# Scores from 64-row halves, batch 0's K and Q kept on chip, and a new place for the first six search steps

## The chip, the cores and the metric

The kernel runs on one core of one Trainium2 chip. The metric is the device time of one launch in microseconds: 1080.16 us, the median of three runs (1077.16 to 1082.32). A profile of one more execution, with its trace, is what the text below reads.

## The reference, cut to what matters

```python
# q, k, v: [4 batches, 8 heads, 576 tokens, 64]
scores = q @ k.T / 8
kth = the 32nd largest of each row
attn = softmax(scores where scores >= kth, else -1e9)
x = (attn @ v), as [2304 tokens, 512]
h = x @ w_in;            x = max(0.01 * h, h) @ w_out        # 512 -> 2048 -> 512
h = max(x @ w1, x @ w2, x @ w3);  out = h @ w_out2           # 512 -> 768 -> 512
```

Everything is float32 or wider at the boundary; the weights come as float64 bits.

## The kernel before

Every operand of a matmul is split into two float16 parts, a high and a low one, so that products keep nearly float32 accuracy: three or four matmuls for one.

**Attention** works in *steps*. The tokens of a batch are cut into four full blocks of 128 (F0 to F3) and a half block of 64 (HB); the heads come in four pairs (`hp`). A full step is one block and one head pair: 128 query rows, both heads side by side, 576 scores each. A half step is the half block and two head pairs: 64 rows of one head and 64 of another share the 128 partitions. Batch 0 goes F0, HB, F1, F2, F3, so its steps 0 to 3 are F0, 4 and 5 are HB, and 6 to 17 are F1 to F3. There are 72 steps, 64 of them full. One step (`attention`, L685):

- TensorE makes the scores of head j=0 into PSUM (L707), ScalarE evicts them into S (L712), then the same for j=1. There is one score buffer in PSUM and three S buffers.
- VectorE searches the 32 largest of each row: MAX8 (L722) four times and MATCH_REPLACE8 (L724) three times, for both heads. A head's search starts when its own eviction is done.
- ScalarE and POOL make the exponentials, their sums' factors and the high and low parts (L732 to L756); a DMA transposes them (L757); TensorE multiplies by V (L783 to L785); ScalarE scales by the row sum.
- When a block's last head pair is done, a second DMA transposes its tokens into the buffer of a *unit* (`xu<-xhl`, L819).

In the scores both halves of q and k are stacked on the 128 contraction rows: for one head, k's tile holds the high part in rows 0 to 63 and the low part in rows 64 to 127, and q's tile is there twice, once as high over low and once as low over high (`st`). Two matmuls of 128 rows then give all four products. To get these layouts, `prep_qk` (L372) splits q and k of each batch and head pair, writes the parts to DRAM (L394, two DMAs each), and `load_k` (L411, one DMA) and `load_q` (L419, L422, three DMAs per block) read them back.

**Units** are the token groups of the feed-forward part (`ffn`, L846), ten of them: 192 tokens (F0 and HB of batch 0), 128 (F1), then 256 (unit 2 is F2 and F3 of batch 0) seven times, and 192. A unit does `h<-xu,wi` and `acc<-f16t,wo` (the first two matrices), then `h<-k,w` and `acc<-f16t,w` (the other two stages), 672 matmuls in all, three for each product (`three`, L824). Unit 0 waits for all of `w_in` and `w_out`, and its second half for all of the others.

**Weights** come as float64 and are converted on VectorE in chunks, three integer operations for 512 columns (L501, L504, L507), then scaled and split by ScalarE and POOL (`prep_w`, L475). `prep_w` is called for 8 chunks of `w_in`, 8 of `w_out`, 6 of w1 to w3 and 4 of the last matrix.

**Order.** All this is entered into a planner (`Plan`, L75) as operations with an engine, an estimated length, what they read and write, and a priority. The planner lays the operations out by these estimates, engine by engine, taking what can start earliest and among those the lower priority; the program then has that order on every engine, and each engine works through its list in order. A search step i has priority TP(i) (L678): 0, 2, 4 and 6 for the first NE=4 steps, then 10 + 11.9 i, which is 57.6 and 69.5 for steps 4 and 5. The chunks have priorities from 2.0 on, 2.1 apart for `w_in` (to 16.7), 1.5 for `w_out` (18.8 to 29.3), and end near 47. So steps 4 and 5 stand behind all weights.

SP issues all DMAs from one list, in order.

Of the kernel before, what the change touches and what calls it, by code (L numbers as in the profile page):

```python
# [36 lines left out]
VC = 11  # L37
# [15 lines left out]
NE = 4  # L53
TE = 0.0
TS = 2.0
# [5 lines left out]
class Buf:  # L61
    def __init__(self, tag, make):
        self.tag, self.make, self.ap, self.left, self.seq, self.also = tag, make, None, 0, None, ()
        self.done, self.emit = None, 0
        self.last = 0.0
# [9 lines left out]
class Plan:  # L75
# [50 lines left out]
    def run(self):  # L126
# [11 lines left out]
        while len(order) < total:  # L138
            best = None
            for e, lst in pend.items():  # L140
                t0 = free[e]
                cand = None
                for n in lst:
                    t, ok = max(n.ready, t0, lanes[-8] if e == SP else 0.0), True
                    need = {}
                    for b in n.bufs:
                        if b.ap is None and b.last == 0.0 and not getattr(b, "on", False):
# [6 lines left out]
                            t = max(t, sl[k] + 0.2)  # L154
                    if not ok:
# [78 lines left out]
def attention_moe_kernel(ctx, tc, qk, v, w_in, w_out, w123, w2o, outT):  # L234
# [9 lines left out]
    NB = {"xu": 2, "raw": 2, "hl": 1, "k2": 7, "kt": 4, "qt": 2, "vt": 4, "S": 3, "w": 1, "m": 2, "nb": 2, "nt": 2, "pp": 1,  # L244
# [46 lines left out]
    NCOL = 318  # L291
# [80 lines left out]
    def prep_qk(b, hp, pr, fast):  # L372
        d = dr.tile([2, 2, 2, D, S], F16, name=f"dqk{b}_{hp}")
# [3 lines left out]
        for a in (1, 0):  # L377
# [31 lines left out]
    def load_k(b, hp, pr):  # L409
        k = buf("kt", [P, 2, S], F16)  # L410
        op(SP, 0.55, lambda: Y.dma_start(k(), DQK[b, hp][1].rearrange("h r d s -> (r d) h s")),  # L411
           r=[("d", b, hp, 1, 0), ("d", b, hp, 1, 1)], w=[k], pr=pr, dma=dma(P * 2 * S * 2))
        KT[b, hp] = k

    def load_q(b, hp, t0, n, pr):
        q = buf("qt", [P, 2, 2, P], F16)
        rd = [("d", b, hp, 0, 0), ("d", b, hp, 0, 1)]
        src = DQK[b, hp][0]
# [724 lines left out]
```

## Time and profile before

| | |
|---|---|
| median of three runs | 1080.16 us |
| the profiled execution's own time | 1078.56 us |
| its span on the core | 1076.6 us |
| TensorE (PE) busy | 903.1 us, 84% |
| VectorE (DVE) busy | 875.2 us, 81% |
| ScalarE (ACT) busy | 835.2 us, 78% |
| GpSimd (POOL) busy | 600.5 us, 56% |
| DMA, all queues | 125.78 MB, mean 117 GB/s |

Times in rows are microseconds from the span's start, unless marked ns. L707 is line 707 of the kernel before. A matmul's row gives its start and how long it was in flight; matmuls overlap, so the rate is read from start to start. `128*128` or `128*64` in a matmul's row is the part of the array that it uses: contraction rows by output columns. PEld is TensorE's weight load, SPq the queue of SP that issues DMAs. The page's slices are fortieths of the span, about 27 us each.

### The profile page before, as it was taken

How to read it: one execution, taken by the hardware profiler on the slowest of the kernel's cores; microseconds unless marked ns; L12 is line 12 of the kernel's file. 1: busy time of each engine (PE TensorE's matmuls, PEld its weight loads, DVE VectorE, ACT ScalarE, POOL GpSimd, SP SyncE). 2: the span in 40 equal slices, each digit the busy share in tenths (PEclk: the TensorE clock that was granted, in tenths of full speed). 3: DMA queues.
4: the chain of work that ended last, by engine and by line, in shares of the span. 5: the costliest groups of instructions: out<-in, count | busy, mean ns of one | idle time of the engine just before them, and what ended most of it. 6: DMA issues, size and time to landing. Idle time of an engine off the chain costs nothing.

```text
span 1076.6 us, 27391 instructions
## 1 busy us (share of the span) xinstructions
PE 903.1 (84%) x10292; PEld 795.0 (74%) x10292; DVE 875.2 (81%) x2010; ACT 835.2 (78%) x1769; POOL 600.5 (56%) x1110
## 2 busy tenths in 40 slices
PE   3343334688999998998999899989999999999998
PEld 2231223577988887887888798878878897888998
DVE  5899999999998999999459999999389999900101
ACT  7777878999888888689879868987887788664242
POOL 5355766776476655467655545666754555443131
PEclk9985556789999999999999999999999999999999
DMA  8968447547755443355763334663833343220000
GB/s 283 310 147 277 162 110 247 158 111 150 129 106 118 100 89 68 77 125 127 143 173 82 80 76 98 155 123 88 173 80 88 79 90 85 65 60 2 21 2 16
DMA packets 268516, 125.78 MB, mean 117 GB/s; under 512 B 237408, under 2 KB 255328, under 8 KB 266336
## 3 DMA queue, kind: packets, MB, share of 16 engines
q1 hardware_dynamic: 268384, 124.04, 47.4%
q8 instruction: 81, 1.33, 0.5%
q14 instruction: 51, 0.42, 0.1%
HBM read 62.65 MB, written 14.16 MB: 71 GB/s over the span
## 4 chain that ended last, share of the span: by engine, by line
PE 42%; ACT 18%; DVE 10%; DMA 7%; POOL 6%; issue 5%; SPq 1%; POOLq 0%; ACTq 0%; DVEq 0%
PE h L825 7%; PE h L826 7%; PE h L827 7%; PE acc L825 5%; PE acc L826 5%; PE acc L827 5%; DMA pt<-phl 3%; DVE m L722 3%; PE s L707 3%; POOL phl L754 3%; DVE w L724 3%; ACT pp L749 3%; ACT pp L746 2%; ACT S L712 2%; DMA raw<-in_v 2%
## 5 line engine op out<-in xcount | busy, mean ns | idle before, releaser
L722 DVE MAX8 m<-w 128x8 f32<-128x576 f32 x432 | 308.8, 748 | 0.3
L886 POOL TENSOR_TENSOR f16t<-k,f16t 128x256 f16<-128x256 f32 (+2 forms) x220 | 136.9, 624 | 211.2 <-ACT f16t L880 193.1
L754 POOL TENSOR_TENSOR phl<-pp,phl 128x576 f16<-128x576 f32 x144 | 183.5, 1282 | 85.3 <-ACT phl L752 83.2
L724 DVE MATCH_REPLACE8 w<-m,w 128x576 f32<-128x576 f32 x288 | 212.4, 743 | 0.0
L825 PE MATMUL h<-k,w 128*128 128x256 f16 (+2 forms) x720 | 186.4, 263 | 7.7 <-ACT k L926 5.5
L826 PE MATMUL h<-k,w 128*128 128x256 f16 (+2 forms) x720 | 186.3, 263 | 3.4 <-POOL k L928 3.0
L827 PE MATMUL h<-k,w 128*128 128x256 f16 (+2 forms) x720 | 186.3, 263 | 0.0
L826 PE MATMUL acc<-f16t,wo 128*128 128x256 f16 (+2 forms) x640 | 165.8, 263 | 3.7 <-POOL f16t L886 3.7
L825 PE MATMUL acc<-f16t,wo 128*128 128x256 f16 (+2 forms) x640 | 166.0, 263 | 0.7 <-ACT f16t L880 0.6
L827 PE MATMUL acc<-f16t,wo 128*128 128x256 f16 (+2 forms) x640 | 165.9, 263 | 0.0
L825 PE MATMUL h<-xu,wi 128*128 128x256 f16 (+1 forms) x576 | 155.9, 271 | 3.2 <-DMA xu<-xhl 1.9
L827 PE MATMUL h<-xu,wi 128*128 128x256 f16 (+1 forms) x576 | 156.0, 271 | 0.0
L826 PE MATMUL h<-xu,wi 128*128 128x256 f16 (+1 forms) x576 | 156.0, 271 | 0.0
L707 PE MATMUL s<-kt,qt 128*128 128x288 f16 (+5 forms) x800 | 106.2, 281 | 46.1 <-ACT S L712 31.8
L746 ACT ACTIVATE pp<-S,nt 128x576 f32<-128x576 f32 x144 | 107.9, 771 | 32.7 <-POOL nt L732 24.8
L880 ACT ACTIVATE f16t<-k 128x256 f16<-128x256 f32 (+2 forms) x220 | 86.9, 396 | 56.3 <-DVE k L970 53.7
L749 ACT ACTIVATE pp<-pp,nb,colt 128x576 f32<-128x576 f32 x144 | 123.7, 866 | 0.1
L722 DVE MAX8 m<-S 128x8 f32<-128x576 f32 x144 | 103.5, 746 | 19.1 <-ACT S L712 19.0
L707 PEld LDWEIGHTS <-qt 128*128 128x128 f16 (+1 forms) x800 | 62.3, 106 | 66.3 <-issue 41.9
L873 ACT ACTIVATE k<-h,colt 128x256 f32<-128x256 f32 (+2 forms) x160 | 72.4, 455 | 48.0 <-PE h L827 47.4
L826 PEld LDWEIGHTS <-w 128*128 128x128 f16 x960 | 94.2, 98 | 17.4 <-issue 9.2
L724 DVE MATCH_REPLACE8 w<-m,S 128x576 f32<-128x576 f32 x144 | 106.4, 743 | 0.0
(132 smaller groups left out, 2507.6 us busy)
## 6 DMA issues: line engine op xcount, KB each, us to landing
rw<-in_w SPq DMA_DIRECT2D x18, 512.0 KB, 5.5
w<-in_w_in SPq DMA_DIRECT2D x8, 1024.0 KB, 7.2
w<-in_w_out SPq DMA_DIRECT2D x8, 1024.0 KB, 5.6
raw<-in_qk SPq DMA_DIRECT2D x24, 288.0 KB, 3.5
dqk<-hl SPq DMA_DIRECT2D x48, 144.0 KB, 2.7
kt<-dqk SPq DMA_DIRECT2D x16, 288.0 KB, 3.0
qt<-dqk SPq DMA_DIRECT2D x144, 32.0 KB, 2.2
raw<-in_v SPq DMA_DIRECT2D x12, 352.0 KB, 3.4
```

The costliest lines, as they stand in the source:

```text
L707: T.matmul(p()[osl, h, o:o + w], q()[:, hh, st, :n], k()[:, hh, kc:kc + w], start=st == 0, stop=st == 1, skip_group_check=True)
L722: op(DVE, dve(S), lambda mc=mc, src=src: V.max(mc(), src()), r=rd, w=[(m, j, 0, r)], pr=pd)
L724: op(DVE, dve(S) + 0.06, lambda mc=mc, src=src, j=j: V.match_replace(out=wp()[:, j], in_to_replace=mc(), in_values=src(), imm_value=NEG), ...
L746: op(ACT, act(S, aps=1), lambda j=j: A.activation(pp()[:, j], Sb[j](), AF.Prelu, bias=nt()[:, j:j + 1], alpha=STEEP), r=[(Sp, j), nt], w=[ ...
L749: op(ACT, act(S, aps=2), lambda j=j, es=es: A.activation(pp()[:, j], pp()[:, j], AF.Exp, bias=nb()[:, j:j + 1], scale=es), r=[(nb, j), ((" ...
L754: op(POOL, pool(S), lambda j=j: G.tensor_tensor(phl()[:, 1, j], pp()[:, j], phl()[:, 0, j], op=ALU.subtract), r=[(pp, j), (phl, 0, j)], w= ...
L825: T.matmul(out, wt(0), xt(0), start=first, stop=False, skip_group_check=True)
L826: T.matmul(out, wt(0), xt(1), start=False, stop=False, skip_group_check=True)
L827: T.matmul(out, wt(1), xt(0), start=False, stop=last, skip_group_check=True)
L873: op(ACT, act(N, True, 1), lambda: A.activation(rr()[:, 0, :N], p()[:, :N], AF.Prelu, scale=SC["e"][:, c:c + 1], alpha=0.01), r=[p, "e_in" ...
L880: op(ACT, act(N), lambda: A.activation(hl()[:, 0, :N], g()[:, 0, :N], AF.Copy), r=[(g, 0)], w=[(hl, 0)], pr=pr)
L886: op(POOL, pool(N), lambda: G.tensor_tensor(hl()[:, 1, :N], g()[:, 0, :N], hl()[:, 0, :N], op=ALU.subtract), r=[(g, 0), (hl, 0)], w=[(hl, ...
```

## The change

- **Scores.** k's and q's tiles now have both heads of a pair on the 128 rows, head 0 in rows 0 to 63 and head 1 in rows 64 to 127, and the high and the low part side by side. One matmul contracts over 64 rows; four of them (high and low of q by high and low of k, `x` and `y`) add up in PSUM. The score group is now one half of the columns (`c`, 288) of both heads instead of all columns of one: for a full step 8 matmuls of 288 columns, the heads in turn, for a half step 16. The eviction takes a column half of both heads, and a head's search starts when both evictions are done. In half steps the two partition halves belong to two head pairs and not to two heads of one; their scale factors are put into one column by two small POOL copies.
- **Columns.** The second head's keys are rotated by 64 tokens on the host, as the kernel before did by three matmuls of 64, 224 and 288 columns. V loses one of 11 padded column groups.
- **DRAM round trips.** The parts are written in one DMA instead of two, q's block is read in one instead of three. For batch 0, k's parts stay in the buffer that the scores read, and nothing is written or read; q's parts are read where they lie for the first block (F0) and go through DRAM for the other four.
- **Plan.** The first six steps get the priorities 0, 4, 8, 12, 16 and 20 (NE=6, TS=4.0), so steps 4 and 5 stand among the last chunks of `w_in` and the first of `w_out`. And an operation that uses a buffer which another has already taken is not laid out before the buffer came free (`since`).

```diff
-VC = 11
+VC = 10
-NE = 4
+NE = 6
-TS = 2.0
+TS = 4.0
...
+                        else:
+                            t = max(t, b.since)
...
-                    slots[b.tag].pop(0)
+                    b.since = slots[b.tag].pop(0) + 0.2
...
 def prep_qk(b, hp, pr, fast):
-        d = dr.tile([2, 2, 2, D, S], F16, name=f"dqk{b}_{hp}")
+        d = dr.tile([2, P, 2, S], F16, name=f"dqk{b}_{hp}")
...
-            hl = buf("hl" if b else "ph", [P, 2, S], F16)
+            hl = buf("hl" if b else "kt" if a else "ph", [P, 2, S], F16)
...
-            for h in range(2):
-                op(SP, 0.55, lambda hl=hl, a=a, h=h: Y.dma_start(d[a, h].rearrange("r d s -> d r s"),
-                                                               hl()[h * D:(h + 1) * D]),
-                   r=[(hl, 0), (hl, 1)] + z0, w=[("d", b, hp, a, h)], pr=pr, dma=dma(P * S * 2))
+            if b == 0 and a:
+                KT[b, hp] = hl
+                continue
+            if b == 0:
+                QT[b, hp, ORDER[0][0][0]] = hl
+            op(SP, 0.55, lambda hl=hl, a=a: Y.dma_start(d[a], hl()), r=[(hl, 0), (hl, 1)] + z1, w=[("d", b, hp, a)],
+               pr=pr, dma=dma(P * 2 * S * 2))
...
 def load_q(b, hp, t0, n, pr):
-        q = buf("qt", [P, 2, 2, P], F16)
-        op(SP, 0.55, lambda: Y.dma_start(q()[:, :, 0, :n], src[:, :, :, t0:t0 + n].rearrange("h r d s -> (r d) h s")),
-           r=rd, w=[(q, 0)], pr=pr, dma=dma(P * 2 * n * 2) + 0.2)
-        for r in range(2):
-            op(SP, 0.55, lambda r=r: Y.dma_start(q()[r * D:(r + 1) * D, :, 1, :n],
-                                                src[:, 1 - r, :, t0:t0 + n].rearrange("h d s -> d h s")),
-               r=rd, w=[(q, 1 + r)], pr=pr, dma=dma(P * n * 2) + 0.2)
+        if (b, hp, t0) in QT:
+            return
+        q = buf("qt", [P, 2, P], F16)
+        op(SP, 0.55, lambda: Y.dma_start(q()[:, :, :n], DQK[b, hp][0][:, :, t0:t0 + n]), r=[("d", b, hp, 0)],
+           w=[(q, 0), (q, 1)], pr=pr, dma=dma(P * 2 * n * 2) + 0.2)
...
 def attention(i):
-        for j in range(2):
-            k, q = KT[b, hps[j]], QT[b, hps[j], t0]
+        pairs = [(slice(0, n), hps[0])] if full else [(slice(0, 64), hps[0]), (slice(64, P), hps[1])]
...
+        for c in range(2):
             p = buf("s", [P, 2, 512])
-            hs = [(j, slice(0, P))] if full else [(0, slice(0, 64)), (1, slice(64, P))]
-            cols = ((0, 0, 0, 288), (1, 0, 288, 288)) if j == 0 else \
-                   ((0, 0, 512, 64), (0, 64, 0, 224), (1, 0, 224, 288))
-            def qk_(p=p, k=k, q=q, hs=hs, cols=cols):
-                for h, o, kc, w in cols:
-                    for hh, osl in hs:
-                        for st in range(2):
-                            T.matmul(p()[osl, h, o:o + w], q()[:, hh, st, :n], k()[:, hh, kc:kc + w],
-                                     start=st == 0, stop=st == 1, skip_group_check=True)
+            def qk_(p=p, c=c):
+                for x in range(2):
+                    for y in range(2):
+                        for h in range(2):
+                            hx = slice(D * h, D * h + D)
+                            for o, hp in pairs:
+                                T.matmul(p()[o, h, :288], QT[b, hp, t0]()[hx, x, QO(b, t0):QO(b, t0) + n],
+                                         KT[b, hp]()[hx, y, 288 * c:288 * c + 288], start=x + y == 0, stop=x + y == 2,
+                                         skip_group_check=True)
...
-                rd = [(Sp, j)] if g < 2 else [(wp, j, 0)]
+                rd = sk if g < 2 else [(wp, j, 0)]
```

## Rows read from the trace of the kernel before

**Rows 1.** Busy tenths of TensorE in 40 slices, from the page.
```profile
PE   3343334688999998998999899989999999999998
```

**Rows 2.** Stages: us, then busy us of PE, PEld, DVE, ACT, POOL; clock, DMA.
```profile
22.50:316.60 294.10, 171.34 (x2015) 145.55 (x2014) 284.42 (x641) 249.14 (x486) 180.01 (x304) 0.77 0.66 177
349.00:944.00 595.00, 570.41 (x6406) 500.20 (x6407) 538.61 (x1241) 490.28 (x1060) 348.27 (x635) 1.00 0.47 103
944.00:1076.60 132.60, 126.64 (x1398) 118.27 (x1396) 12.10 (x32) 50.35 (x129) 38.31 (x71) 0.99 0.07 18
```

**Rows 3.** Timeline where unit 2 starts: start, us, engine, line, operation, idle before.
```profile
346.16 1.24 SPq L819 DMA_TRANSPOSE xu<-xhl  x1
...
348.53 0.22 PE L827 MATMUL acc<-f16t,w 128*128 128x128 f16 x1
...
349.10 0.28 PE L825 MATMUL h<-xu,wi 128*128 128x256 f16 x1 [0.35 <-DMA xu<-xhl]
```

**Rows 4.** MAX8 of L722 alone, from the start to 316.6 us.
```profile
0.00:316.60 316.60, 101.99 (x145) 0.79 0.68 185
```

**Rows 5.** Timeline of the first 24 us, around the first scores.
```profile
6.39 1.55 DVE L362 SCALAR_TENSOR_TENSOR wo<-wo,colt 128x576 f16<-128x576 f32 x2 [0.38 <-ACT wo L361]
...
7.34 2.79 SPq L394 DMA_DIRECT2D dqk<-wo  x4
...
17.16 1.26 SPq L422 DMA_DIRECT2D qt<-dqk  x2
...
20.32 1.16 PE L707 MATMUL s<-kt,qt 128*128 128x288 f16 x4
...
21.81 0.63 ACT L712 ACTIVATE S<-s 128x576 f32<-128x576 f32 x1
...
22.48 0.76 DVE L722 MAX8 m<-S 128x8 f32<-128x576 f32 x1
```

**Rows 6.** VectorE alone between its first work and the first MAX8.
```profile
12.65:22.48 9.83, 4.48 (x10) 1.00 0.86 256
```

**Rows 7.** Timeline of TensorE where unit 0 starts.
```profile
186.66 0.34 PE L825 MATMUL h<-xu,wi 128*128 128x192 f16 x1 [1.52 <-DMA xu<-xhl]
```

**Rows 8.** Groups of VectorE: operation, shapes, count, busy us, mean ns, idle before.
```profile
L724 DVE MATCH_REPLACE8 w<-m,w 128x576 f32<-128x576 f32 x288 | 212.4, 743 | 0.0
...
L507 DVE SCALAR_TENSOR_TENSOR w<-w,acc 128x512 int32<-128x512 int32 x32 | 21.6, 678 | 0.0
...
L501 DVE TENSOR_SCALAR acc<-w 128x512 int32<-128x512 int32 x32 | 20.7, 684 | 3.7 <-DMA w<-in_w_in 3.7
```

**Rows 9.** Timeline of TensorE: a score group of a full step.
```profile
565.60 0.27 PE L827 MATMUL acc<-f16t,wo 128*128 128x256 f16 x1
565.71 0.65 PE L707 MATMUL s<-kt,qt 128*128 128x288 f16 x4
566.20 0.27 PE L825 MATMUL acc<-f16t,wo 128*128 128x256 f16 x1
```

**Rows 10.** The same for a score group of a half step.
```profile
477.37 0.27 PE L827 MATMUL acc<-f16t,wo 128*128 128x256 f16 x1
477.57 0.68 PE L707 MATMUL s<-kt,qt 128*64 128x288 f16 x8
478.19 0.28 PE L825 MATMUL acc<-f16t,wo 128*128 128x256 f16 x1
```

**Rows 11.** Groups of TensorE by shape, 349 to 944 us.
```profile
L707 PE MATMUL s<-kt,qt 128*128 128x288 f16 x254 | 45.6, 287 | 4.0 <-ACT S L712 3.1 <-DMA qt<-dqk 0.8
...
L707 PE MATMUL s<-kt,qt 128*128 128x224 f16 x86 | 15.5, 262 | 0.0
```

**Rows 12.** Waits of TensorE from 349 us on: us, times, longest.
```profile
PE s L707 <- ACT S L712: 7.4, 10, 1.7
...
PE s L707 <- DMA qt<-dqk: 1.7, 3, 0.9
```

**Rows 13.** DMA issues: count, KB each, median us to landing.
```profile
qt<-dqk SPq DMA_DIRECT2D x144, 32.0 KB, 2.2
```

**Rows 14.** Group of POOL: the low part of V.
```profile
L367 POOL TENSOR_TENSOR vt<-raw,vt 128x704 f16<-128x704 f32 x12 | 17.8, 1484 | 5.2 <-ACT vt L366 5.1
```

More of the change, by code (lines that the diff above doesn't have):

```diff
@@ L64, in __init__ @@
         self.done, self.emit = None, 0
-        self.last = 0.0
+        self.last = self.since = 0.0
     def __call__(self):
@@ L460, in ones_ @@
             G.memset(t()[:, :, 64:65], 1.0)
-            for c, lo in ((8, 64), (9, 0), (10, 64 if hp % 2 == 0 else 0)):
+            for c, lo in ((8, 64), (9, 0)):
                 G.memset(t()[lo:lo + 64, c, 64:65], 0.0)
@@ L679, in TP, with QO @@
         return TE + TS * i if i < NE else TA0 + TA * i
+    def QO(b, t0):
+        return t0 if b == 0 and t0 == ORDER[0][0][0] else 0
     RLAG = 2.0
@@ new lines, in attention @@
+        esk = [(("es", b, hp), 1) for _, hp in pairs]
+        es = ES[b, hps[0]]
+        if not full:
+            if (b, hps) not in ES:
+                use_ring(("esc", b % 2, hps[0]), 1)
+                ES[b, hps] = col()
+                use_ring()
+                for x, hp in pairs:
+                    op(POOL, 0.2, lambda x=x, hp=hp: G.tensor_copy(ES[b, hps][x], ES[b, hp][x]),
+                       r=[(("es", b, hp), 1)], w=[("esc", b, hps, hp)], pr=pr)
+            es, esk = ES[b, hps], [("esc", b, hps, hp) for hp in hps]
@@ new lines, in attention @@
+        for c in range(2):
+            p = buf("s", [P, 2, 512])
+            def qk_(p=p, c=c):
[7 more added lines that the diff above has]
+                                         skip_group_check=True)
+            op(PE, 0.5 * (COLD if i < NCOLD else 1), qk_,
+               r=[(z[b, hp, *v], x) for _, hp in pairs for z, v in ((KT, ()), (QT, (t0,))) for x in range(2)]
+               + (["ZO"] if b == 0 and t0 == ORDER[0][0][0] else []), w=[p], pr=pq)
+            op(ACT, act(S, True), lambda c=c, p=p: A.activation(Sp()[:, :, 288 * c:288 * c + 288], p()[:, :, :288],
+                                                               AF.Copy), r=[p], w=[(Sp, c)], pr=pq)
@@ L714, in attention @@
+        sk = [(Sp, 0), (Sp, 1)]
         tk = lambda j: [(m, j, 0, 3)]
@@ L735, in attention @@
            r=tk(0) + tk(1) + [(m, 0, 0, 0), (m, 1, 0, 0)], w=[(nb, 0), (nb, 1)], pr=pr)
[L736 to L743 removed]
+        op(POOL, 0.28, lambda: G.tensor_scalar(nb(), nb(), es, LNPS, op0=ALU.mult, op1=ALU.add), r=esk,
+           w=[(nb, 0), (nb, 1)], pr=pr)
         for j in range(2):
[L745 removed]
             op(ACT, act(S, aps=1), lambda j=j: A.activation(pp()[:, j], Sb[j](), AF.Prelu, bias=nt()[:, j:j + 1],
                                                             alpha=STEEP),
[L748 to L749 removed]
+               r=sk + [nt], w=[(pp, j)], pr=pr)
+            op(ACT, act(S, aps=2), lambda j=j: A.activation(pp()[:, j], pp()[:, j], AF.Exp,
                                                                    bias=nb()[:, j:j + 1], scale=es),
[L751 removed]
+               r=[(nb, j)] + esk, w=[(pp, j)], pr=pr)
             op(ACT, act(S), lambda j=j: A.activation(phl()[:, 0, j], pp()[:, j], AF.Copy),
@@ L771, in avm @@
             def avm(j=j, vt=vt):
-                hs = [(j, slice(0, P), j)] if full else [(hh, slice(64 * hh, 64 * hh + 64), 2 * j + hh)
+                hs = [(j, slice(0, P), j)] if full else [(hh, slice(64 * j, 64 * j + 64), 2 * j + hh)
                                                         for hh in range(2)]
@@ L777, in avm @@
                         if c < 4:
-                            ch, k = c + 5 * j, 2 * c + hh
+                            ch, k = c + 5 * hh, 2 * c + hh
                         else:
-                            ch, k = 4, 8 + hh if hh == j else 10
+                            ch, k = 4, 8 + hh
                         hc, lc = pt()[:, 0, ch, qs], pt()[:, 1, ch, qs]
```

40 lines of the change are left out of this document (12 added, 28 removed).

## Prediction

> **What bounds the kernel now.** I read the slices of the page first: TensorE is at three or four tenths until about slice 8 and at nine from then on, up to the end [rows 1]. The table by stages says the same in numbers: from 349 to 944 us TensorE is busy for 570 of 595 us, VectorE for 539; after 944 VectorE has nothing left and TensorE runs 127 of 133 us. Before, from 22.5 to 316.6 us, the full engine is VectorE: 284.4 of 294.1 us, while TensorE has 171 [rows 2]. So there are two stages with different limits, and the timeline shows where one hands over to the other: the first matmul of unit 2 (256 tokens, blocks F2 and F3 of batch 0) starts at 349.10 and is released by the DMA that brings its tokens (`xu<-xhl`, issued at 346.16), half a microsecond after unit 1's last matmul at 348.53 [rows 3]. Those tokens need the eighteenth search step, and VectorE has done its 18 x 8 MAX8 by 316.6 [rows 4]. From unit 2 on TensorE is short of hardly anything. The time is therefore (start of unit 2) + (TensorE's work from there, some 728 us). I price each part by which of the two it moves.
>
> **The start: Q and K of batch 0 stay on chip.** Today the split of head pair 0 is done at 7.94 (6.39 + 1.55) on VectorE, goes out from 7.34, comes back by loads that are issued up to 18.4; the first scores start at 20.32 and the first MAX8 at 22.48 [rows 5]. After the change K is used where it was split and the first block's Q too, so the scores can start at about 8.1. From first matmul to first MAX8 it is 2.2 us today (22.48 - 20.32); now both column halves must be evicted, and the second half adds a group of 1.16 us and an eviction of 0.63 us [rows 5], 2 us with the semaphores: first MAX8 at about 12.3. What this is worth is VectorE's idle time that search work fills: between 12.65 and 22.48 it is busy for 4.48 of 9.83 us [rows 6], so 5.4 us. Later steps hide the second eviction behind three S buffers.
>
> The 18 steps are then done at 316.6 - 5.4 = 311. From there to unit 2 it takes 32.5 us today (349.1 - 316.6); unit 1's last phases, whose VectorE and ScalarE work lies in just this stretch, will have moved ahead, so I take 27 and get 338. Bounds: VectorE without any of its remaining 9.7 us of idle time [rows 2], and 27 us, give 328 (21 gained); the same lag and 3 us lost to unit 1's work in front of step 18 give 347 (2 gained). I take **11 us gained**.
>
> **The start: six steps before w_out.** Steps 4 and 5, and with them unit 0, now stand in front of `w_out` and the last two matrices. Unit 0's first matmul is at 186.66 today, released by its tokens [rows 7]. VectorE's work that must precede it is six steps of about 10.6 us (5.7 us of MAX8, 101.99 over 18 [rows 4], six MATCH_REPLACE8 of 0.743 [rows 8] and what little lies between) and the conversion of `w_in` and `w_out`, three operations x 32 of 0.68 us, 20.7 + 21.6 + a middle one of the same kind, 63 us [rows 8]: 127 us from 12.5 on, so unit 0 can start near 145 to 150. It is not in the sum: the order changes, VectorE's total up to step 18 does not, and unit 2 waits for that total. What it buys is that units 0 and 1 are out of the way by then, used above. If unit 1 were not done, nothing would be gained.
>
> **Scores in 64-row halves.** Before, a full step is two groups on TensorE, 4 matmuls of 288 columns and 6 of 64, 224 and 288; after, two groups of 8 of 288 columns over 64 rows, head 0 and head 1 in turn. If each pair overlaps, a group streams the same columns as now. The trace shows no 64-row tile; the nearest rows are the half steps, whose 128 x 64 tiles already run in pairs. A 128-row group without a wait: 565.60 the matmul ahead, 565.71 the first score, 566.20 the next other matmul: 0.11 + 0.49 us [rows 9]. A group of 8 in 64-column tiles: 477.37, 477.57, 478.19: 0.20 + 0.62 us [rows 10]. The 8 overlap in pairs, or 288 columns x 8 would need 0.98 us, twice the 0.49 of four; but entering and leaving the tiled form costs 0.22 us more than a plain group.
>
> The Trainium skill ("TensorEngine Tiling (Array Packing)", Key Properties) says that changing the tiling mode drains TensorE, whichever way the array is cut. The trace agrees for column tiles, as those 0.22 us; of row tiles no run here shows anything, and by the rule alone the chance of the first rival below falls.
>
> Bounds: 0 us (row tiles drain nothing) to 0.22 + 0.49 us a group (pairs don't overlap). I take 0.22, the value of the nearest row. Unit 2's stretch holds 86 matmuls of 224 columns, two per full step, so 43 full steps [rows 11]: 43 x 2 x 0.22 = **19 us added**, on the path, as TensorE waits for little there (7.4 us for score evictions, 1.7 us for loads of q [rows 12]). The full steps ahead of unit 2 pay too, but TensorE has 123 us free there [rows 2]. Half steps go from pairs to fours of the same columns and are tiled already: nothing.
>
> Another sentence of the same skill points against the change: "TensorE: Matmul & The Clock Gate", Part 3, has a measured 3.07x for four row tiles, 77% of four. As an estimate by that page, pairs at 77% would add 0.15 us to each group's 0.49, some 13 us in all, and the sum would be 1099; no run here shows it.
>
> **The small edits.** Loads of q fall from 240 issues (144 and 64 of full blocks and 32 of half blocks, [rows 13] has the first) to 76, the round trips of k go for batch 0 and the writes come in one piece: that is time of SP's queue and of DMA, and TensorE waits 1.7 us for q in its own stretch [rows 12], so at most that. V of 640 instead of 704 columns saves a tenth of 1.48 us on POOL [rows 14], 16 times, off the path. The combined scale column of half steps adds a few tiny POOL operations, hidden in POOL's idle time (180 of 294 us busy [rows 2]). The planner's rule that a buffer's later users wait for it too changes no work.
>
> **Sum.** Against the profiled execution's own 1078.56 us (span 1076.6 and 2 us around it): - 11 + 19 = 1086.6. That execution is 1.6 us under the median of 1080.16; I forecast **1087**.
>
> **Rivals.**
> 1. *Row tiles enter and leave without a drain.* Then only the start counts: 1078.6 - 11 = 1068, faster. It decides where a group costs under 0.13 us more than now (11 / 86). For it: no row shows a row tile, and they use all 128 columns. Against: column tiles pay both ways in every group.
> 2. *The start gains more*: VectorE loses none of its 9.7 us, unit 2 at 328: 1078.6 - 21 + 19 = 1077, no change. For it: those 9.7 us, and a lag of 32.5 us that other work stretches. Against: VectorE is already at 97% there [rows 2], and its work up to step 18 stays.
> 3. *The start gains nothing*: the weights' DMA or ScalarE holds the eighteenth step where it is, or unit 1 is late. 1078.6 + 19 - 2 = 1096. For it: ScalarE is busy 249 of 294 us [rows 2] and takes over more work early.
> 4. *The pairs overlap in part or not at all*: 0.1 to 0.49 us more per group, 9 to 42 us: 1096 to 1129. For it: two heads write two halves of PSUM at once, which no group does now. Against: column tiles overlap fully [rows 10].
>
> **How the numbers follow.** About 5.4 us (0.5%) is what a measurement of this kernel tells from no change. Forecast (1083 to 1091) 0.36, of it 0.11 under 1085.6; rival 1 0.20; rival 2 0.19, of it 0.05 as a gain that can be measured; rival 3 0.14; rival 4 0.11. Faster 0.20 + 0.05 = 0.25; same 0.11 + 0.14 = 0.25; slower the rest, 0.50. The range takes in rivals 1 and 3 with some room and leaves out the upper part of rival 4: 1064 to 1106; the forecast's own is 1083 to 1091.
>
> **What would show it.** First MAX8 at 12 to 13 us; first matmul of unit 0 near 150; 18 x 8 MAX8 done near 311; unit 2's first matmul near 338, released by its tokens; a full step's group of 8 with 0.20 us ahead of it and 0.62 us to the next other matmul; from unit 2 to the end some 745 us. The forecast is wrong if a group of 8 takes 0.11 + 0.49 us (rival 1) or over 1 us (rival 4), or if unit 2 starts outside 328 to 347.

## The result, and the profile after

| | before | after |
|---|---|---|
| median of the runs made together (4 each) | 1081.24 us | 1097.37 us (1094.17 to 1100.3) |
| ratio, 95% interval | | 1.0147 [1.0103, 1.0191] |
| the profiled execution, its span | 1078.56, 1076.6 us | 1100.3, 1098.5 us |

The change makes the kernel slower by about 16 us. The sign was forecast and 1097 lies in the range of 1064 to 1106, but the forecast was + 7, and 1097 lies outside the forecast's own range of 1083 to 1091.

The page's slices of TensorE look as before [rows 1], and in the line of its chain of waits by engine, line and share the transposed exponentials (`pt<-phl`) now take 7%; before it was 3%.

```profile
PE   4343447569999989998999799999999998999998
...
PE h L838 9%; PE h L839 8%; PE h L840 8%; DMA pt<-phl 7%; PE acc L838 5%; PE s L724 5%; PE acc L839 5%; PE acc L840 5%; DVE m L742 3%; POOL phl L767 3%; DVE w L744 3%; PE h L796 2%; PE h L797 2%; ACT pp L762 1%; PE h L798 1%
```

The stages of the changed kernel, columns as in [rows 2], are bounded by its own unit 0, step 18, unit 2, its VectorE's last work and its end:

```profile
154.40:316.00 161.60, 124.13 (x1606) 109.19 (x1607) 154.32 (x352) 144.97 (x316) 105.73 (x199) 0.86 0.57 146
316.00:347.70 31.70, 26.97 (x408) 23.46 (x406) 27.28 (x70) 26.89 (x64) 20.38 (x48) 0.89 0.49 102
347.70:966.00 618.30, 590.30 (x6757) 490.02 (x6758) 541.65 (x1247) 498.34 (x1061) 346.91 (x627) 0.99 0.43 93
966.00:1098.50 132.50, 124.98 (x1382) 116.64 (x1379) 12.10 (x32) 49.10 (x125) 36.63 (x69) 1.00 0.10 20
```

The handover answers to [rows 3], in the timeline around unit 2's first matmul. Unit 1's last matmul starts at 345.39; a score group waits for ScalarE's eviction; then unit 2 starts at 347.68, again released by its tokens. That is 1.4 us earlier than before and not 11.

```profile
343.82 1.23 SPq L832 DMA_TRANSPOSE xu<-xhl  x1
...
345.39 0.22 PE L840 MATMUL acc<-f16t,w 128*128 128x128 f16 x1
346.60 0.67 PE L724 MATMUL s<-kt,qt 64*128 64x288 f16 x8 [1.00 <-ACT S L731]
347.68 0.40 PE L838 MATMUL h<-xu,wi 128*128 128x256 f16 x1 [0.41 <-DMA xu<-xhl]
```

So the loss lies behind that point: the stretch from unit 2's first matmul to the last matmul of unit 9, the *stage* below, is 746.8 us (347.7 to 1094.5); before it was 723.4 (349.1 to 1072.5). In it TensorE is busy for 18.2 us more and idle for 5.2 us more; the two rows are the stage before and after, columns as in [rows 2].

```profile
349.10:1072.50 723.40, 697.05 (x7802) 618.47 (x7802) 550.61 (x1273) 539.65 (x1185) 386.48 (x705) 1.00 0.39 87
...
347.70:1094.50 746.80, 715.29 (x8136) 606.66 (x8136) 553.75 (x1279) 546.58 (x1183) 383.54 (x695) 0.99 0.37 80
```

The two profiled executions lie 21.9 us apart and the medians 16.1: the one after is the slowest of its four, and the one before lies 2.7 us under its median. So a few microseconds between two traces can be the executions' own.

**The start.** The first scores begin at 7.13 and 7.98 (K's low part is awaited), as forecast (8.1). But the first eviction comes at 12.87, the second at 14.73, and the first MAX8 at 15.41 and not at 12.3. The timeline of the first 16 us shows what ScalarE did: its list has the squares of the next head pair (`junk<-wo`) ahead of the eviction, and the first of them waited 3.49 us for its input.

```profile
7.13 0.66 PE L724 MATMUL s<-kt,wo 64*128 64x288 f16 x4 [1.33 <-ACT wo L363]
...
7.98 0.66 PE L724 MATMUL s<-kt,wo 64*128 64x288 f16 x4 [0.19 <-DVE wo L364]
...
10.57 0.68 ACT L356 ACTIVATE junk<-wo 128x576 bf16<-128x576 f32 x1 [3.49 <-DMA wo<-in_qk]
...
12.87 0.63 ACT L731 ACTIVATE S<-s 128x576 f32<-128x576 f32 x1
...
14.73 0.65 ACT L731 ACTIVATE S<-s 128x576 f32<-128x576 f32 x1
...
15.41 0.76 DVE L742 MAX8 m<-S 128x8 f32<-128x576 f32 x1
```

VectorE's window that was half idle [rows 6] is filled all the same; the second row is a later stretch of the same answer, in which VectorE had been busy for 126.20 us before:

```profile
12.65:22.48 9.83, 9.34 (x23) 1.00 0.70 255
...
187.00:316.60 129.60, 123.34 (x288) 0.88 0.55 136
```

Of the 4.9 us of idle time that this window loses, 2.9 us come back in that stretch and 2.2 us ahead of the window, in the first 12.65 us, where VectorE is busy for 3.91 us and was for 6.08. The MAX8 of the 18 steps, which answer to [rows 4], end at 316.0 (forecast: 311), and unit 0 starts at 154.41 (forecast: near 150), 32 us earlier than before [rows 7]:

```profile
0.00:316.00 316.00, 103.00 (x145) 0.80 0.61 173
```

```profile
154.41 0.32 PE L838 MATMUL h<-xu,wi 128*128 128x192 f16 x1
```

**The score groups.** The timeline of TensorE around a full step's group, and around a half step's, answers to [rows 9] and [rows 10]. Ahead of the group of 8 there are 0.20 us (361.17 to 361.37), from its first matmul to the next other one 0.60; before, 0.11 and 0.49. The median of such groups in the stage is 205 ns from the start of the matmul ahead to the group's first, 381 from its first start to its last, and 215 from there to the next other matmul; the plain group of 4 before had 109, 367 and 122. So a group costs 0.20 us more. The half step's group of 16 takes what the 8 took.

```profile
361.17 0.27 PE L840 MATMUL h<-xu,wi 128*128 128x256 f16 x1
361.37 0.66 PE L724 MATMUL s<-kt,qt 64*128 64x288 f16 x8
361.97 0.28 PE L838 MATMUL h<-xu,wi 128*128 128x256 f16 x1
...
487.23 0.27 PE L840 MATMUL h<-xu,wi 128*128 128x256 f16 x1
487.43 0.68 PE L724 MATMUL s<-kt,qt 64*64 64x288 f16 x16
488.04 0.28 PE L838 MATMUL acc<-f16t,wo 128*128 128x256 f16 x1
```

By shape, from 347.7 to 966 us, there are 688 matmuls of full steps, 86 groups of 8 as counted [rows 11]:

```profile
L724 PE MATMUL s<-kt,qt 64*128 64x288 f16 x688 | 57.9, 288 | 4.4 <-ACT S L731 3.6 <-DMA qt<-dqk 0.7
```

And TensorE waits for something that it hardly waited for before (0.5 us in 2 waits from 349.1 on, beneath those of [rows 12]): the transposed exponentials. Waits of TensorE from 347.7 us on:

```profile
PE h L796 <- DMA pt<-phl: 7.9, 11, 1.7
```

### The profile page after: what moved, and what is told of

Same layout as the page of the kernel before. It is cut to its first block, busy times and chain, and to the rows that moved or that the text cites. A ratio compares the mean times of both kernels' runs of the same rounds, so it can differ in the third digit from the quotient of the medians.

```text
span 1098.5 us, 27981 instructions
## 1 busy us (share of the span) xinstructions
PE 930.1 (85%) x10772; PEld 782.5 (71%) x10772; DVE 875.7 (80%) x2010; ACT 842.7 (77%) x1769; POOL 597.7 (54%) x1102
## 4 chain that ended last, share of the span: by engine, by line
PE 51%; ACT 12%; DVE 11%; DMA 9%; POOL 7%; issue 5%; SPq 0%; POOLq 0%; ACTq 0%; DVEq 0%
PE h L838 9%; PE h L839 8%; PE h L840 8%; DMA pt<-phl 7%; PE acc L838 5%; PE s L724 5%; PE acc L839 5%; PE acc L840 5%; DVE m L742 3%; POOL phl L767 3%; DVE w L744 3%; PE h L796 2%; PE h L797 2%; ACT pp L762 1%; PE h L798 1%
## 5 line engine op out<-in xcount | busy, mean ns | idle before, releaser
L724 PE MATMUL s<-kt,qt 64*128 64x288 f16 (+1 forms) x1216 | 101.4, 311 | 40.5 <-ACT S L731 34.3
L759 ACT ACTIVATE pp<-S,nt 128x576 f32<-128x576 f32 x144 | 107.2, 767 | 21.8 <-POOL nt L752 18.5
L796 PE MATMUL h<-vt,pt 128*128 128x65 f16 (+1 forms) x800 | 89.7, 201 | 25.6 <-DMA pt<-phl 21.4
L838 PEld LDWEIGHTS <-w 128*128 128x128 f16 x960 | 96.1, 100 | 17.4 <-issue 10.1
L839 PEld LDWEIGHTS <-w 128*128 128x128 f16 x960 | 94.4, 98 | 18.8 <-issue 11.3
## 6 DMA issues: line engine op xcount, KB each, us to landing
raw<-in_qk SPq DMA_DIRECT2D x24, 288.0 KB, 3.3
dqk<-hl SPq DMA_DIRECT2D x24, 288.0 KB, 2.5
kt<-dqk SPq DMA_DIRECT2D x12, 288.0 KB, 3.1
```

The lines of the kernel that those rows point to most:

```text
L724: T.matmul(p()[o, h, :288], QT[b, hp, t0]()[hx, x, QO(b, t0):QO(b, t0) + n], KT[b, hp]()[hx, y, 288 * c:288 * c + 288], start=x + y == 0, ...
L759: op(ACT, act(S, aps=1), lambda j=j: A.activation(pp()[:, j], Sb[j](), AF.Prelu, bias=nt()[:, j:j + 1], alpha=STEEP), r=sk + [nt], w=[(pp, ...
L796: T.matmul(o, hc, vh, start=c == 0, stop=False, skip_group_check=True)
L838: T.matmul(out, wt(0), xt(0), start=first, stop=False, skip_group_check=True)
L839: T.matmul(out, wt(0), xt(1), start=False, stop=False, skip_group_check=True)
```

## The experiments

Each kernel was timed beside the kernel before, whose median was 1080.95 to 1081.62 us. Parts are priced by the ratios, times 1081.24 us; the change as a whole is + 15.9 us by its ratio. "Unit 2" is the start of its first matmul, "18 steps" the end of the eighteenth step's last MAX8, "busy" TensorE's busy time in the stage as the profile counts it, all in the profiled execution; the rest of the stage is TensorE's idle time. By names and shapes, sinceonly has the instructions of the kernel before in the same order on every engine (but for 2 of 10292 matmuls), and newplan has those of sixonly. Each of these pairs is in effect one kernel traced twice, and its columns differ by up to 1.6 us.

| kernel | median us | ratio, 95% | 18 steps | unit 1 ends | unit 2 | stage us | busy us | `pt` waits in the stage, us |
|---|---|---|---|---|---|---|---|---|
| before | | | 316.7 | 348.7 | 349.1 | 723.4 | 697.1 | 0.5 |
| after | 1097.37 | 1.0147 [1.0103, 1.0191] | 316.0 | 345.6 | 347.7 | 746.8 | 715.3 | 7.9 |
| rows128 | 1088.16 | 1.0056 [1.0035, 1.0078] | 313.9 | 344.2 | 346.5 | 737.1 | 700.1 | 11.9 |
| coltiles | 1097.25 | 1.0154 [1.0122, 1.0187] | 320.2 | 352.7 | 353.1 | 736.9 | 713.0 | 1.8 |
| newplan | 1087.85 | 1.0062 [1.0039, 1.0084] | 320.0 | 342.5 | 354.1 | 726.8 | 696.1 | 6.6 |
| sinceonly | 1080.67 | 0.9994 [0.9978, 1.001] | 315.5 | 347.7 | 347.9 | 724.4 | 698.0 | 0.8 |
| sixonly | 1087.32 | 1.0055 [1.0039, 1.0071] | 320.9 | 343.4 | 355.1 | 727.2 | 697.7 | 5.5 |
| oldsteps | 1089.32 | 1.0081 [1.0051, 1.011] | 307.8 | 341.2 | 341.8 | 741.7 | 714.8 | 5.3 |
| viadram | 1106.37 | 1.0217 [1.0194, 1.024] | 321.9 | 354.4 | 354.2 | 746.4 | 716.2 | 6.4 |
| regroup | 1088.47 | 1.0062 [1.0041, 1.0084] | 320.8 | 357.1 | 355.3 | 727.0 | 696.9 | 10.0 |
| hybrid | 1091.81 | 1.0093 [1.0073, 1.0112] | 311.6 | 350.0 | 351.8 | 732.9 | 699.2 | 8.1 |
| short | 1058.36 | 0.9785 [0.9762, 0.9808] | 300.1 | 337.5 | 338.5 | 715.6 | 695.5 | 2.2 |
| hybridshort | 1073.68 | 0.9937 [0.9915, 0.9959] | 288.0 | 329.4 | 329.3 | 732.9 | 697.3 | 13.2 |

**rows128: are the 64-row halves what slows the stage?** The changed kernel with the same groups, columns and plan, but each group as 4 matmuls over all 128 rows, which add both heads' products.

```diff
-                        for h in range(2):
-                            hx = slice(D * h, D * h + D)
-                            for o, hp in pairs:
-                                T.matmul(p()[o, h, :288], QT[b, hp, t0]()[hx, x, ...],
-                                         KT[b, hp]()[hx, y, 288 * c:288 * c + 288], ...)
+                        for o, hp in pairs:
+                            T.matmul(p()[o, y, :288], QT[b, hp, t0]()[:, x, ...],
+                                     KT[b, hp]()[:, y, 288 * c:288 * c + 288], ...)
```

> The changed kernel with the score groups in the old 128-row form: for each pair of 64-row matmuls one matmul over all 128 rows, 4 instead of 8 in a full step's group. It leaves out the separation of the two heads (each score is a sum over both), everything else, plan, buffers, transfers and the length that the planner takes for a group, is as in the changed kernel. Theory (entering and leaving the tiled form is what costs): a full group goes back from about 0.20 + 0.60 us to 0.11 + 0.49, unit 2 to the end from 747 to about 727 us, and the time to 1076 to 1082 us, the kernel before within 0.5%. Rival (the new order of the plan costs it, for instance TensorE waiting for the transposed exponentials): the time stays above 1088 us and unit 2 to the end above 738 us.

1.0056 instead of 1.0147: the row tiles cost some 9.8 us of the whole, 9.7 of the stage. The theory (at most 1082) missed; the time lies just inside the rival's bound of 1088, the stage just outside its 738. Its timeline of a full step's group is that of the kernel before, 0.11 and 0.49 us:

```profile
379.66 0.27 PE L838 MATMUL h<-xu,wi 128*128 128x256 f16 x1
379.77 0.66 PE L722 MATMUL s<-kt,qt 128*128 128x288 f16 x4
380.26 0.27 PE L836 MATMUL h<-xu,wi 128*128 128x256 f16 x1
```

So 86 groups should have given back 86 x 0.20 = 17 us. On TensorE they nearly did: its busy time in the stage falls by 15.2 us. But its idle time there rises by 5.5 us, to 37.0. With groups that end sooner it waits longer, 4.0 us of it for the exponentials (11.9 us; 7.9 with the tiles). On the other engines the instructions stand in the order of the changed kernel. The stage, and the wait:

```profile
346.50:1083.60 737.10, 700.11 (x7696) 616.70 (x7696) 553.04 (x1279) 543.33 (x1183) 382.50 (x695) 0.99 0.38 81
...
PE h L794 <- DMA pt<-phl: 11.9, 13, 1.9
```

And the rest stays: rows128 has plain groups, and a stage of 737.1 us, 13.7 more than before. Of these, 10.6 us are idle time of TensorE and 3.1 us busy time.

**coltiles: the price of tiles alone.** The kernel before, its full steps' scores as pairs of 64-column tiles.

```diff
+                hc = [(j_, slice(64 * x, 64 * x + 64), slice(64 * x, 64 * x + 64) if full else slice(0, n))
+                      for x in range(2) for j_ in [hs[min(x, len(hs) - 1)][0]]]
...
-                    for hh, osl in hs:
-                        for st in range(2):
-                            T.matmul(p()[osl, h, o:o + w], q()[:, hh, st, :n], k()[:, hh, kc:kc + w],
+                    for st in range(2):
+                        for hh, osl, qs in hc:
+                            T.matmul(p()[osl, h, o:o + w], q()[:, hh, st, qs], k()[:, hh, kc:kc + w],
```

> The kernel before, with every 128-row score matmul of a full step cut into two of 64 output columns, in pairs as the half steps have them; same numbers, same plan, nothing on chip. Theory (any tiled form drains TensorE on the way in and out, 0.22 us a group): 43 x 2 x 0.22 = 19 us more from unit 2 to the end, 1095 to 1103 us in all, as slow as the changed kernel. Rival (the price belongs to the row tiles, or is hidden in waits): under 1088 us.

1.0154, or 16.7 us, as the theory had it. In the trace 13.5 us lie in the stage and 4.0 ahead of unit 2, where the prediction put the groups at nothing. The timeline has 0.20 us ahead of the group and 0.63 to the next matmul, which is what the row tiles show too:

```profile
382.74 0.27 PE L829 MATMUL h<-xu,wi 128*128 128x256 f16 x1
382.94 0.69 PE L709 MATMUL s<-kt,qt 128*64 128x64 f16 x12
383.57 0.28 PE L827 MATMUL h<-xu,wi 128*128 128x256 f16 x1
```

Either cut of the array pays the same entry and exit. In the stage TensorE is busy for 15.9 us more than before, of the 19 forecast for the stage, and idle for 2.4 us less.

**newplan, sinceonly, sixonly: the plan in the kernel before.** newplan has NE=6, TS=4.0 and the rule `since`; the other two have one of them each.

```diff
-NE = 4
+NE = 6
-TS = 2.0
+TS = 4.0
...
+                        else:
+                            t = max(t, b.since)
...
-                    slots[b.tag].pop(0)
+                    b.since = slots[b.tag].pop(0) + 0.2
```

> The kernel before with the plan's part of the change alone: six early steps, 4.0 apart, and the rule that later users of a buffer wait for it. Theory (VectorE's total up to step 18 sets unit 2's start, and the order doesn't change it): unit 0 starts at 150 to 160 us, unit 2 between 344 and 354, the time within 0.5% of the kernel before. Rival (the order itself helps): unit 2 before 340 us and the time under 1075. Rival (the order itself costs the 16 us): over 1090 us.

> The kernel before with one part of the plan's change, the rule that a buffer's later users wait for it too; the first steps' priorities are the old ones. The plan's change as a whole cost 6.9 us (5 us later to unit 2, the rest as TensorE's wait for transposed exponentials: 6.6 us against 0.5). Theory (the order of the early steps holds up unit 2, and the rule shifts later waits): 1082 to 1086 us, unit 2 within 2 us of the kernel before, TensorE's wait for the transposed exponentials above 4 us. Rival (the rule alone is the whole loss): 1086 to 1091 and unit 2 at 352 or later. Rival (the rule is harmless): within 2 us of the kernel before, that wait under 2 us.

> The kernel before with the other part of the plan's change: the six early steps at 4.0 apart, without the rule on buffers. Theory (putting steps 4 and 5 ahead of the other weights doesn't lessen VectorE's total up to step 18 and delays the weights' chain): unit 0 starts at 150 to 162 us, unit 2 at 350 to 356, the time 1082 to 1087. Rival (the early steps are free and the rule was the loss): 1076 to 1082 and unit 2 at 346 to 350.

newplan is slower by 6.7 us, sixonly by 5.9, sinceonly by nothing. The rule leaves the order as it was, alone and beside the six steps, so newplan and sixonly are one test made twice: the six early steps cost some 6 us in a kernel in which nothing else is changed. Of the expectations, newplan's (within 0.5%) missed narrowly, sixonly's theory held to 0.3 us, and for sinceonly the rival that the rule is harmless held. The work is as the prediction says: up to the eighteenth step VectorE is busy for 294.4 to 295.8 us in all kernels with the same conversions. What differs is its idle time. One row each, VectorE from the start to that step, first of the kernel before:

```profile
0.00:316.60 316.60, 295.00 (x664) 0.79 0.68 185
```

sixonly, 25.3 us idle where before has 21.6:

```profile
0.00:320.90 320.90, 295.58 (x666) 0.79 0.66 183
```

The changed kernel, 21.3:

```profile
0.00:316.00 316.00, 294.69 (x664) 0.80 0.61 173
```

and oldsteps (next), 13.1:

```profile
0.00:307.80 307.80, 294.69 (x664) 0.92 0.62 178
```

In sixonly unit 1 is done 5 us earlier (343.4), as the prediction had it, and it buys nothing: unit 2 starts 11.7 us after it. In between TensorE waits, in its list's order, for other things. Its waits from 342 to 356 us, and its timeline there:

```profile
PE s L707 <- ACT S L712: 4.8, 3, 3.4
PE h L325 <- ACT junk L811: 3.1, 1, 3.1
```

```profile
346.67 0.59 PE L325 MATMUL h<-colt,ones 128*128 128x1 f32 x2 [3.10 <-ACT junk L811]
350.62 1.12 PE L707 MATMUL s<-kt,qt 128*128 128x64 f16 x6 [3.36 <-ACT S L712]
352.48 1.12 PE L707 MATMUL s<-kt,qt 128*128 128x288 f16 x4 [0.75 <-ACT S L712]
...
355.06 0.35 PE L825 MATMUL h<-xu,wi 128*128 128x256 f16 x1
```

ScalarE, in the same stretch, makes the eviction for which the scores wait only after the exponentials of an older step, and these waited for their factors from POOL:

```profile
347.83 1.44 ACT L746 ACTIVATE pp<-S,nt 128x576 f32<-128x576 f32 x2 [1.21 <-POOL nt L732]
349.18 0.85 ACT L749 ACTIVATE pp<-pp,nb,colt 128x576 f32<-128x576 f32 x1
349.94 0.63 ACT L712 ACTIVATE S<-s 128x576 f32<-128x576 f32 x1
```

That fits S buffers that are all taken until `pp<-S` has read one, but no run has a fourth S buffer, so it stays a reading.

**oldsteps: the six steps in the changed kernel.** NE=4 and TS=2.0 put back.

```diff
-NE = 6
+NE = 4
-TS = 4.0
+TS = 2.0
```

> The changed kernel with the first four steps at 0, 2, 4 and 6 and steps 4 and 5 behind the weights again, as before; 64-row scores, K and Q on chip and the rule on buffers stay. Theory (the 64-row groups cost 9 to 16 us, and the early steps some 3 to 5 of the rest): 1090 to 1096 us. Rival (the early steps are what pays in the changed kernel): 1098 or more. Rival (the early steps are the plan's whole loss): under 1090.

1.0081: 7.1 us better than the change as it is, and by its median the rival holds that the early steps are the plan's whole loss. The eighteenth step ends at 307.8 and unit 2 starts at 341.8, that is 8.9 and 7.3 us earlier than before: without the early steps, much of the start gain of the prediction is there in this kernel (unit 2 was forecast at 338). In its stage TensorE is busy for 17.7 us more than before and idle for as long (26.9 us; 26.4 before). So this kernel does nearly what the prediction's two terms say: they make + 8, and it is at + 8.8.

**viadram: what keeping batch 0 on chip is worth.** The changed kernel with batch 0 through DRAM like the others.

```diff
-            hl = buf("hl" if b else "kt" if a else "ph", [P, 2, S], F16)
+            hl = buf("hl" if b else "ph", [P, 2, S], F16)
...
-            if b == 0 and a:
-                KT[b, hp] = hl
-                continue
-            if b == 0:
-                QT[b, hp, ORDER[0][0][0]] = hl
```

> The changed kernel with batch 0's k and q going through DRAM as the other batches' do; 64-row scores and the new plan stay. Theory (K and Q on chip let the first search start at 15.4 instead of some 22 us, but VectorE's total up to step 18 is what counts, so it is worth the idle time filled, 3 to 6 us): first MAX8 at 21 to 24 us, unit 2 at 349 to 354, the time 1099 to 1104. Rival (it is worth nothing): within 2 us of the changed kernel's 1097. Rival (it is worth the whole 7 us or more): over 1105.

1.0217: 7.6 us worse than the change, by its time the rival of 7 us or more; unit 2 is 6.5 us later, and the stage is the same (746.4). The timeline of its start has the first scores waiting for the load and the first MAX8 at 25.32, 9.9 us later than in the changed kernel:

```profile
21.57 1.14 PE L715 MATMUL s<-kt,qt 64*128 64x288 f16 x8 [6.72 <-DMA qt<-dqk]
...
25.32 1.42 DVE L733 MAX8 m<-S 128x8 f32<-128x576 f32 x2
```

**regroup: groups of column halves, without tiles, on-chip parts and early steps.** Groups of one column half of both heads and a search that waits for both evictions; 128-row matmuls, DRAM and the old steps as before. It is made from the changed kernel, so the rest of the change is in it too: the rule `since`, the combined scale column, V of 640 columns, and a third q buffer, which the change has besides what its section lists.

```diff
-        for j in range(2):
-            k, q = KT[b, hps[j]], QT[b, hps[j], t0]
+        for c in range(2):
...
+                    for h in range(2):
+                        for st in range(2):
+                            for o, hp in pairs:
+                                T.matmul(p()[o, h, :288], QT[b, hp, t0]()[:, h, st, :n],
+                                         KT[b, hp]()[:, h, 288 * c:288 * c + 288], ...)
...
+            op(ACT, act(S, True), lambda c=c, p=p: A.activation(Sp()[:, :, 288 * c:288 * c + 288],
+                                                               p()[:, :, :288], AF.Copy), ...)
```

> The kernel before with the regrouping alone: score groups and evictions by column halves of both heads, a search that waits for both evictions, second head's keys rotated, V of 640 columns, three q buffers; 128-row matmuls, all batches through DRAM, the old places of the first steps, the rule on buffers (which alone moved nothing). The 128-row form of the changed kernel needs 737 us from unit 2 to the end, the kernel before 723; the early steps alone bring 4 of these 14. Theory (the regrouping brings the other 9 to 10: the search gets its scores later and the plan sets the transposed exponentials tight before their matmuls): unit 2 to the end 731 to 735 us, the time 1086 to 1092. Rival (it is free, and the 9 come with K and Q on chip or from early steps and regrouping together): 723 to 727 us and 1078 to 1084.

1.0062, or 6.7 us: unit 2 6.2 us later, the stage 3.6 longer, and `pt` waits of 10.0 us in place of 0.5. The time is in the theory's range, the stage in the rival's. The stage's 3.6 us are idle time of TensorE, and as unit 2 starts before unit 1 has ended, a little of unit 1's work is in it. That the groups are the cause is not shown: the other parts of the change were not run alone, apart from the rule.

**short: is VectorE's total what sets unit 2?** The kernel before without the middle one of the three conversions, 20.9 + 12.0 + 4.4 us of VectorE; the weights lose their three lowest mantissa bits.

```diff
-                        (dve(cw), lambda w=w, m=m: V.scalar_tensor_tensor(
-                            m(), w()[:, :, 0], 29, m(), op0=ALU.logical_shift_right, op1=ALU.bitwise_or),
-                         [raw] + zr + zf, [pb]),
```

> The kernel before without the middle one of the three integer operations in which VectorE converts a weight chunk: the three lowest bits of a float32 weight are left out (20 bits of the mantissa stay). It takes 58 operations of 0.64 to 0.69 us, about 38 us, from VectorE ahead of unit 2 and nothing from any other engine. Theory (VectorE's total up to step 18 sets unit 2's start): step 18's search is done some 33 to 38 us earlier, unit 2 starts at 312 to 325 us instead of 349 and the time falls to 1046 to 1058. Rival (ScalarE, DMA or unit 1 holds unit 2 where it is): unit 2 after 338 us and the time above 1070.

0.9785, or 23.2 us faster, the best of all kernels here. The time is at the edge of the theory's range, and unit 2 is where the rival has it: with 33 us less work up to the eighteenth step (261.92 us, after 295.00), that step ends only 16.6 us earlier, and unit 2 starts only 10.6 us earlier, a microsecond after unit 1's end. The other part of the trace's gain of 18.5 us is a stage that is 7.8 us shorter (715.6 us), 6.2 of it idle time of TensorE. From unit 2 to the end of the span:

```profile
338.50:1058.10 719.60, 695.46 (x7804) 617.51 (x7801) 545.42 (x1260) 541.21 (x1185) 384.45 (x699) 1.00 0.40 88
```

**hybrid, hybridshort: only the gain.** hybrid is the changed kernel with the old steps, batch 0 as changed, and the scores of the other three batches per head over 128 rows, loaded as before; hybridshort leaves the middle conversion out as well.

```diff
+                if b:
+                    for h in range(2):
+                        for st in range(2):
+                            for o, hp in pairs:
+                                T.matmul(p()[o, h, :288], QT[b, hp, t0]()[:, c, st, :n],
+                                         KT[b, hp]()[:, c, 288 * h:288 * h + 288], ...)
+                    return
```

> Batch 0 as in the changed kernel (64-row scores by column halves, K and the first Q on chip), batches 1 to 3 as in the kernel before (128 rows, a group and an eviction for each head, through DRAM), the old places of the first steps. Theory (on-chip K and Q bring unit 2 forward by some 7 us, and the tiled form costs only in the stage that TensorE bounds, which batch 0 hardly reaches): unit 2 at 340 to 344 us, 723 to 728 us from there, the time 1072 to 1077. Rival (the gain of the start is given back in the later stage, as the plan changes): 1079 to 1084.

> The hybrid (batch 0 on chip in 64-row form, batches 1 to 3 as before, old places of the first steps) without the middle one of the three operations in which a weight chunk is converted, which leaves out a weight's three lowest bits. Without it alone the kernel before took 1058 us, 22.6 less, of which unit 2 started 10.6 earlier. Theory (both shorten VectorE's work ahead of unit 2, so they add up): 1048 to 1054 us. Rival (with the middle operation gone VectorE is no longer what holds unit 2, and the two don't add up): 1056 to 1060.

Both theories missed, and so did both rivals by their numbers; hybrid's stage is longer, as its rival has it, but its gain is gone ahead of the stage already. In hybrid the eighteenth step ends 5 us earlier than before (311.6), but unit 1 1.3 us later and unit 2 2.7 us later; and the stage, in which the scores are those of the kernel before, takes 9.5 us longer, with 8.1 us of `pt` waits. Batch 0 is treated as in oldsteps, and yet unit 2 starts 10.0 us later than there. So the parts don't add up freely: what else is in the plan moves unit 2 by as much as the change itself.

## Why the prediction was half right

1. **The start gain (- 11) is the step that failed; - 1.4 came.** The mechanism is there: keeping batch 0 on chip moves unit 2 by 6.5 us and the time by 7.6 (viadram against after), the size of the 5.4 us and the shorter lag, and with the old steps unit 2 starts 7.3 us earlier than before (oldsteps). What takes it back is the six early steps, which the prediction left out of its sum: they move unit 2 by 5.9 us and the time by 7.1 (after against oldsteps), and cost 5.9 to 6.7 us in the kernel before (sixonly, newplan).
2. **"The order changes, VectorE's total up to step 18 does not, and unit 2 waits for that total."** The first half is right (294.7 against 295.0 us of work); the second is wrong. The end of step 18 is the work plus the idle time, and the order sets the idle time: 13.1 us with the old steps, 21.3 with the six. Nor does unit 2 wait for that step alone: in ten of the 13 kernels it starts within 2.4 us of unit 1's end (in newplan and sixonly 11.7 us later, in regroup 1.8 earlier), and short shows that removing work ahead of it helps by a third. That is what rival 3 named ("unit 1 is late", ScalarE "takes over more work early"), at 1096 and with a chance of 0.14; which of the two holds unit 2 in the changed kernel is not shown.
3. **"Later steps hide the second eviction behind three S buffers"** is not settled. regroup loses 6.7 us, 3.6 of them in the stage, but more than the groups is new in it. oldsteps has the same groups, and there unit 2 comes earlier and TensorE's idle time in the stage is as before.
4. **First MAX8 at 12.3: 15.41.** The scores began about a microsecond before they were forecast to; the two evictions were priced by their length, and not by what stood ahead of them in ScalarE's list.
5. **The tiles (+ 19): right in mechanism and nearly in size.** 0.20 us a group instead of 0.22, in 86 groups, is 17 us on TensorE; its busy time in the stage rises by 18.2 us against the kernel before and by 15.2 against rows128. The time that goes away with the tiles is 9.8 us, as TensorE then waits 5.5 us longer in the stage. Rival 1 (no drain) is refuted, and so is rival 4: the 8 matmuls take 381 ns from first to last start where 4 plain ones take 367, so the pairs overlap nearly in full. The Trainium skill ("TensorEngine Tiling (Array Packing)", Key Properties) says that a change of the tiling mode drains TensorE. The 202 to 218 ns on either side of row and column tiles, beside 109 and 122 around plain groups, agree. The Trainium skill ("TensorE: Matmul & The Clock Gate", Part 3) has a measured speedup of 3.07x for four row tiles, 77% of four. This doesn't carry over to these pairs: at 77%, as an estimate by that page, a group would have taken 0.15 us more, and 381 ns beside 367 is 0.014 us more.
6. **"From unit 2 to the end some 745 us".** To the end of the span it is 750.8 us (727.5 before), to the last matmul 746.8 (723.4). Of the 23.4 us more, 18.2 are busy time of TensorE, for which the prediction had 19. The other 5.2 are idle time, which it left as it was without a reason.
7. **Sum by the runs.** The change without the six steps is at + 8.8 us (oldsteps), where the prediction's terms make + 8; the rest of the measured 15.9 us are the six steps. Parts priced in different kernels happen to add up as well: - 7.6 (on chip) + 9.8 (tiles) + 7.1 (six steps) + 6.7 (regroup) + 0 (`since`) = 16.0. That agreement is luck: the first three are differences against the same runs of the changed kernel, whose interval is 4.8 us to either side, oldsteps doesn't show the fourth, and hybrid, which should have kept the first term and shed most of the others, is at + 10.1.
8. **1097 lies in the wide range (1064 to 1106) because that range takes in rival 3's 1096**, not because the forecast's - 11 + 19 came true in this kernel. That rival's sum, - 2 + 19, is close to what came at unit 2 and in TensorE's busy time, but it named other causes: the six early steps are in no rival.

**What stays open** is why TensorE waits longer for the transposed exponentials in the stage: 0.5 us before, 0.8 in sinceonly, 1.8 in coltiles and 2.2 in short, but 5.3 to 13.2 in every kernel whose early steps, groups or first batch were changed. One difference that bears on it is in the traces. The DMA that transposes them is written as before, but takes longer from issue to landing (the last number, a median in us, before and after):

```profile
pt<-phl SPq DMA_TRANSPOSE x72, 4.0
...
pt<-phl SPq DMA_TRANSPOSE x72, 4.7
```

It is 3.9 to 4.3 us in the six kernels with the buffers of the kernel before, and 4.6 to 4.8 in the seven made from the changed kernel, rows128, regroup and both hybrids among them. These seven share V of 640 columns, a third q buffer and more columns for scale factors; which of it lengthens the transfer, and what that costs, no run shows. In newplan and sixonly the waits come with 4.3 and 4.2 us, so it can't be the only cause.

## What to carry to other kernels

Price a tiled group of matmuls by its entry and exit as well as its columns: short groups between plain matmuls pay it every time, and it is seen in full only where no other wait grows when the price goes. So read the engine's busy and idle time apart before calling a part cheap. An order that leaves an engine's total work unchanged still costs: look for the idle time that moves with it, and for what stands ahead of the urgent instruction in each engine's list. When several parts are forecast as zero, run the kernel before with each of them alone, and the changed kernel without each, before adding them up.

## What the runs showed of the hardware

- Entering and leaving a tiled form costs the same for 64-row, 64-column and 64 x 64 tiles: 202 to 205 ns from the start of the matmul ahead to the group's first and 215 to 218 from its last to the next other one, beside 109 and 122 ns for plain groups.
- Two 64-row tiles with different weights run side by side: 8 matmuls of 288 columns in 381 ns from first to last start.
- The same DMA transpose of the exponentials takes 3.9 to 4.3 us to land (median) in six kernels and 4.6 to 4.8 in seven whose other buffers differ; why is not shown.
- The granted clock in the first 150 us differs between executions with the same order of instructions: from 22 to 150 us it is 0.89 in newplan and 0.68 in sixonly, whose profiled executions took 1086.96 and 1088.43 us. The stage runs at 0.99 to 1.00, the 2.4 GHz level, in before, after, rows128, newplan and short.
